# Batch 1's attention split into two groups inside tile 0, a later key-value product for batch 2, and q copies shared with ScalarE

## The chip, the cores and the metric

The kernel runs on one core of a Trainium2 chip. A core has five engines with a queue of instructions each: TensorE (PE, matmuls; PEld are its weight loads), VectorE (DVE), ScalarE (ACT), GpSimd (POOL) and SyncE (SP, which here only issues DMAs). The engines run side by side and wait for each other through semaphores. The metric is the device time of one execution in microseconds, the median of several runs.

## What is computed

Inputs are q, k, v of shape (8 batches, 8 heads, 576 rows, 64) and two weight matrices, 512 x 2048 and 2048 x 512. Cut to what matters:

```python
q_s = softmax(q, axis=-1)            # over the 64 entries of a row
k_s = softmax(k, axis=2)             # over the 576 rows
kv = einsum('bhsd,bhse->bhde', k_s, v)
x = einsum('bhsd,bhde->bhse', q_s, kv)          # "attention", linear in the rows
x = x.transpose(0, 2, 1, 3).reshape(4608, 512)
h = x @ w_in
out = maximum(0.01 * h, h) @ w_out              # 4608 x 512, float32
```

## The kernel before, in words

The 4608 rows are cut into nine tiles of 512 rows, and eight batches of 576 rows supply them. Tile 0 needs batch 0 alone: its layer 1 runs over all 576 rows of batch 0 (first rows 0 to 255, then the 320 others), and the 64 rows too many are carried over to tile 1. Tile 1 then needs the 448 rows behind those, which are the first of batch 1. For tile t >= 1 the body is a loop over 16 column blocks j of layer 1 (`layer1`, line 459, four matmuls each into one PSUM bank; then `leaky` on ScalarE, line 469), then four groups of 128 rows (`tsub`) with 16 layer-2 matmuls each (`layer2`, line 481), each group copied to SBUF and written out by `store` (line 474).

Attention for batch b goes through these steps: maximum of k over the rows (`k_tree`, `k_allmax`, VectorE), subtraction (`k_sub`), exponential (`k_exp`, ScalarE), cast of v (`v_cast`), and the same for q (`q_max`, `q_sub`, `q_exp`, `q_sum`, `q_norm`). `kv` (line 291) is the key-value product: 36 small matmuls into two PSUM banks, half of them for each half of v. `kd_make` (line 309) divides it by k's sums and leaves the matrix kd. q is needed transposed. For batch 0 TensorE does this (`q_transpose`, line 393, into a PSUM tile `psum_qt`) and `q_keep` (line 409) copies it to SBUF, into one tile for each pair of heads (`qT0`, `qT1`; argument `ggs`). From batch 1 on a DMA does it (`q_turn`, line 436). Then attention proper: `attend` (line 417, batch 0) or `attend_x` (line 444, other batches, eight matmuls: four pairs of heads g by two row ranges XR of 320 and 256 rows), each into a PSUM bank and from there, as bf16, into xT, which layer 1 reads. The engine of this copy is an argument.

PSUM has eight banks: two in the pool `psO` and six in `psB` (line 67). In tile 0 layer 2 runs with j outside and the four row groups inside, so that four output sums are open at once: two in `psO`, two in `psB`.

The order of the work is written out by hand. Each engine's queue gets its instructions in the order in which the program issues them. The main loops call `run(t, u)` after step u of tile t, and `at(t, u, ...)` (line 493) registers what is to be issued there. In tile 0 steps 0 to 15 are the column blocks for rows 0 to 255, 16 to 31 those for the other rows, 32 to 47 the j of layer 2. In later tiles 0 to 15 are the column blocks and 16 to 31 are layer 2, four j to a step, so that steps 20 to 23 are the second row group. Within one step the order of registration decides. Before the first loop, layer 1's first halves for blocks 0 to 7 are begun (`begin`, line 659); those for blocks 8 to 15 are begun at j = 8, between the two transposes of batch 0's late rows (lines 673 to 679).

The lines that the change touches: batch 0's late attention (584 to 586), batch 1's attention (597 to 599), batch 2's product and kd (635, 636), `g_carry` (656; eight GpSimd copies of the 64 carried rows), and the `q_keep` calls at j = 8 (677, 679).

Of the kernel before, what the change touches and what calls it, by code (L numbers as in the profile page):

```python
# [25 lines left out]
def kernel(  # L26
# [9 lines left out]
    nc = tc.nc  # L36
# [31 lines left out]
    psO_pool = ctx.enter_context(tc.tile_pool(name="psO", bufs=2, space=bass.MemoryType.PSUM))  # L68
# [75 lines left out]
    def k_begin(b):  # L144
        st[b]["ke"] = ke_pool.tile([P, R, HL, D], BF16, name="ke")
        st[b]["kmax"] = mx_pool.tile([P, HL, D], FP32, name="kmax")
        st[b]["kmaxT"] = mx_pool.tile([P, HL * D], FP32, name="kmaxT")
        st[b]["kall"] = mx_pool.tile([P, HL, D], FP32, name="kall")

    def k_tree(b, hs, steps=slice(0, 4)):  # L150
        n = hs.stop - hs.start
        ks = st[b]["k"][:, hs]
        if steps.start == 0:
            st[b]["t4"] = mx_pool.tile([P, HL, 4, D], FP32, name="t4")[:, 0:n]
        t4 = st[b]["t4"]
        t2, t1 = t4[:, :, 0:2], t4[:, :, 0]
        for o, i0, i1 in (
            (t4, ks[:, :, 0:4], ks[:, :, 4:8]),
            (t2, t2, t4[:, :, 2:4]),
            (t1, t1, t4[:, :, 1]),  # L160
            (st[b]["kmax"][:, hs], t1, ks[:, :, 8]),
        )[steps]:
            nc.vector.tensor_tensor(out=o, in0=i0, in1=i1, op=ALU.max)  # L163

    def k_allmax(b):


        nc.vector.transpose(
            out=st[b]["kmaxT"], in_=st[b]["kmax"].rearrange("p h d -> p (h d)")
        )  # L170
        m2 = small_pool.tile([P, CB, 2], FP32, name="m2")
        nc.vector.tensor_reduce(
            out=m2[:, :, 0],
            in_=st[b]["kmaxT"].rearrange("p (c j) -> p c j", j=32),
            axis=AX.X,
            op=ALU.max,
        )
        for a in range(4):
            o = a ^ 1
            nc.vector.tensor_reduce(  # L180
                out=m2[32 * o : 32 * o + 32, :, 1],
                in_=m2[32 * a : 32 * a + 32, :, 0:1],
                axis=AX.X,
                op=ALU.max,
            )
        m = small_pool.tile([P, CB], FP32, name="m")
        nc.vector.tensor_reduce(out=m, in_=m2, axis=AX.X, op=ALU.max)
        nc.vector.transpose(  # L188
            out=st[b]["kall"].rearrange("p h d -> p (h d)"),
            in_=m.unsqueeze(2).to_broadcast([P, CB, 32]),  # L190
        )
# [27 lines left out]
    def q_begin(b):  # L219
        st[b]["qe"] = qe_pool.tile([P, R, HL, D], BF16, name="qe")  # L220
        if b == 0:
            for gg in range(2):
                st[b]["qT", gg] = qT_pool.tile([P, 2, R, L], BF16, name=f"qT{gg}", tag="qT")
# [67 lines left out]
    def kv(b):  # L291

        pkv = [psB_pool.tile([P, 2, 130], FP32, name="pkv", tag=BANK_TAG) for _ in range(2)]
        for gg in range(2):
            for r in range(R):
                for hh in range(2):
                    rows = slice(hh * L, (hh + 1) * L)
                    nc.tensor.matmul(  # L298
                        pkv[hh][:, gg, 0:129],
                        lhsT=st[b]["ke"][rows, r, 2 * gg : 2 * gg + 2].rearrange(  # L300
                            "p h d -> p (h d)"
                        ),
                        rhs=vb2[b % 2][rows, r, gg, 0:129],
                        start=(r == 0),
                        stop=(r == R - 1),
                    )
        st[b]["pkv"] = pkv

    def kd_make(b):
        for hh in range(2):  # L310
            pkv = st[b]["pkv"][hh]
            krec = small_pool.tile([P, 2, 1], FP32, name="krec")
            nc.vector.reciprocal(out=krec, in_=pkv[:, :, 128:129])
            for hp in range(2):
                p0 = hp * D
                nc.vector.tensor_tensor(
                    out=kd2[b % 2][p0 : p0 + D, 2 * hh : 2 * hh + 2, p0 : p0 + D],
                    in0=pkv[p0 : p0 + D, :, p0 : p0 + D],
                    in1=krec[p0 : p0 + D].to_broadcast([D, 2, D]),
                    op=ALU.mult,  # L320
                )
# [87 lines left out]
    def q_keep(eng, b, r0, n, ggs=(0, 1)):  # L409
        for gg in ggs:  # L410
            o, i = st[b]["qT", gg][:, :, r0 : r0 + n], st[b]["ps", r0][:, gg::2]
            if eng is nc.scalar:
                eng.copy(out=o, in_=i)
            else:
                eng.tensor_copy(out=o, in_=i)

    def attend(b, gs, c0, n, eng, pool=psB_pool, tag=BANK_TAG):

        ps = pool.tile([P, len(gs), n], FP32, name="po", tag=tag)
        for i, g in enumerate(gs):  # L420
            nc.tensor.matmul(
                ps[:, i],
                lhsT=kd2[b % 2][:, g],
                rhs=st[b]["qT", g % 2][:, g // 2].rearrange("c r l -> c (r l)")[:, c0 : c0 + n],
                start=True,
                stop=True,
            )
        x0 = XB[gs[0]]
        o = xT[:, x0 : x0 + len(gs), b * S + c0 : b * S + c0 + n]
        if eng is nc.scalar:  # L430
            eng.copy(out=o, in_=ps)
        else:
            eng.tensor_copy(out=o, in_=ps)
# [10 lines left out]
    def attend_x(b, g, rs, eng):  # L444
        hh, gg = divmod(g, 2)
        n = (rs.stop - rs.start) * L
        ps = psB_pool.tile([P, n], FP32, name="po", tag=BANK_TAG)
        qX = st[b]["qX"].rearrange("c (r g) (h l) -> c g h r l", g=2, h=2)
        nc.tensor.matmul(  # L449
            ps.rearrange("p (r l) -> p r l", l=L), lhsT=kd2[b % 2][:, g], rhs=qX[:, gg, hh, rs]  # L450
        )
        c0 = b * S + rs.start * L
        o = xT[:, XB[g], c0 : c0 + n]
        if eng is nc.scalar:
            eng.copy(out=o, in_=ps)  # L455
        else:
            eng.tensor_copy(out=o, in_=ps)
# [35 lines left out]
    def at(t, u, *fns):  # L493
        while t > 0 and u >= 32:
            t, u = t + 1, u - 32
        hooks.setdefault((t, u), []).extend(fns)
# [14 lines left out]
    XR = (slice(0, 5), slice(5, R))  # L511
# [69 lines left out]
        load_w_out(slice(j0, j1))  # L581


    at(0, 11, lambda: attend(0, [0, 2], 256, 256, nc.scalar))
    at(0, 11, lambda: attend(0, [1, 3], 256, 256, nc.vector))
    at(0, 11, lambda: attend(0, [0, 2, 1, 3], 512, 64, nc.scalar, psO_pool, "pout"))
    at(0, 15, lambda: k_begin(1), lambda: q_begin(1), lambda: k_tree(1, H0), lambda: k_tree(1, H1))
    at(0, 15, lambda: q_max(1, XR[0]), lambda: q_sub(nc.gpsimd, 1, XR[0]), lambda: k_allmax(1))
    at(0, 15, lambda: k_sub(nc.vector, 1, H0), lambda: k_sub(nc.vector, 1, H1))
# [5 lines left out]
    at(0, 39, lambda: kv(1), lambda: q_sum(1, XR[1]), lambda: q_norm(1, XR[1]), lambda: kd_make(1))  # L595
    at(0, 43, lambda: q_turn(1, XR[1]), lambda: load_all(2))
    for i in range(8):
        eng = nc.vector if i in (5, 7) else nc.scalar
        at(0, 47, lambda i=i, eng=eng: attend_x(1, i % 4, XR[i // 4], eng))


    for b in range(3, B):
# [20 lines left out]
    def plan2():  # L623
        b = 2
        at(1, 0, lambda: k_begin(b), lambda: q_begin(b), lambda: k_tree(b, ALLH))
        at(1, 3, lambda: k_allmax(b))
        at(1, 6, lambda: k_sub(nc.vector, b, H0), lambda: k_sub(nc.vector, b, H1))
        at(1, 12, lambda: k_exp(b, ALLH))
        for rs in XR:
            at(1, 9, lambda rs=rs: q_max(b, rs), lambda rs=rs: q_sub(nc.gpsimd, b, rs))  # L630
        at(1, 13, lambda: v_cast(nc.gpsimd, b, 0), lambda: v_cast(nc.gpsimd, b, 1))
        for i, rs in enumerate(XR):
            at(1, (15, 16)[i], lambda rs=rs: q_exp(b, rs), lambda rs=rs: q_sum(b, rs), lambda rs=rs: q_norm(b, rs))
            at(1, (16, 17)[i], lambda rs=rs: q_turn(b, rs))
        at(1, 21, lambda: kv(b))
        at(1, 22, lambda: kd_make(b))
        for i in range(8):
            at(1, 28 + i // 2, lambda i=i: attend_x(b, i % 4, XR[i // 4], nc.scalar))

# [13 lines left out]
            g_next.append(g_tile())  # L653
            nc.gpsimd.tensor_copy(out=g_next[jj][:, :, 0:L], in_=g_sb[jj][:, :, TT : TT + L])

    at(0, 46, g_carry)
    begun = []

    def begin(j):
# [12 lines left out]
    for j in range(0, NF, 2):  # L672
        if j == 8:
            q_transpose(0, 4, 2)
            for jj in range(8, NF, 2):
                begin(jj)
            q_keep(nc.vector, 0, 4, 2)
            q_transpose(0, 6, 3)
            q_keep(nc.vector, 0, 6, 3)
        ph = begun.pop(0)  # L680
        for i in range(2):
            layer1(j + i, ph[:, i], 0, 256, slice(2, 4), i == 0, i == 1)
            if i == 1:
                leaky(g_sb[j // 2][:, :, 0:256], ph)
            run(0, j + i)
# [5 lines left out]
    pout = [psO_pool.tile([P, O], FP32, name="pout") for _ in range(2)]  # L691
# [66 lines left out]
```

## Time and profile before

| what | us |
|---|---|
| median of 3 runs (lowest, highest) | 291.18 (291.14, 291.42) |
| the profiled execution, its own time | 291.04 |
| its span, first to last instruction | 289.2 |
| TensorE busy | 279.7 |
| VectorE, ScalarE, GpSimd busy | 148.5, 148.2, 85.6 |

In the timeline's rows the columns are the start in us from the span's start, the time from the group's start to its end, engine, line, operation, what it writes and reads, the shapes, the number of instructions merged into the row, and in brackets the idle time of the engine just before with what ended it. Rows of the waits give the total in us, the number and the longest. Rows of the chain are the work that ended last, in order of time: start, duration, what. Matmuls overlap, so a group's duration contains the drain of its last matmul, and the next group can start before it ends.

### The profile page before, as it was taken

The numbers are of one execution on the slowest core, as the hardware profiler recorded it, in microseconds if no ns is written. First come the engines' busy times: TensorE is split into PE (matmuls) and PEld (weight loads), VectorE is DVE, ScalarE is ACT, GpSimd is POOL, SyncE is SP. The second block draws the span as 40 slices with busy tenths as digits, with TensorE's granted clock in tenths as the row PEclk, the third lists the DMA queues.
The fourth block names the chain that finished last, engine by engine and source line by source line (L and its number), as shares of the span: only waits on it lengthen the run. The fifth ranks groups of instructions, "written<-read, shape, count | busy, mean of one in ns | idle before, by whom it ended". The sixth has DMA issues, their size and how long they took to land.

```text
span 289.2 us, 4274 instructions
## 1 busy us (share of the span) xinstructions
PE 279.7 (97%) x1646; PEld 138.5 (48%) x1646; DVE 148.5 (51%) x246; ACT 148.2 (51%) x273; POOL 85.6 (30%) x70
## 2 busy tenths in 40 slices
PE   7689999999999999999999999999999999999995
PEld 2277654454444544454454544444454444444443
DVE  3997883896880994388175637554631200110011
ACT  4976870785269307922774358433953066016400
POOL 4735460017059009505900590039100000000000
PEclk9999999999999999999999999999999999999999
DMA  7999996987749174953397239913141310131033
GB/s 257 314 208 378 258 189 186 399 293 296 148 108 399 62 154 118 398 133 76 78 381 187 50 82 348 239 36 73 39 82 36 75 36 1 36 82 29 0 72 75
DMA packets 38932, 46.35 MB, mean 160 GB/s; under 512 B 18304, under 2 KB 21632, under 8 KB 38912
## 3 DMA queue, kind: packets, MB, share of 16 engines
q1 hardware_dynamic: 35456, 41.75, 48.5%
q0 software_dynamic: 3296, 4.20, 8.3%
q8 instruction: 13, 0.21, 0.3%
q10 hardware_dynamic: 160, 0.13, 0.1%
q14 instruction: 7, 0.06, 0.1%
HBM read 36.70 MB, written 9.44 MB: 160 GB/s over the span
## 4 chain that ended last, share of the span: by engine, by line
PE 74%; POOL 1%; ACT 0%; DVE 0%; issue 0%
PE pout L482 37%; PE ph L461 34%; PE pkv L298 2%; PE po L449 2%; POOL vb L216 1%; ACT xT L455 0%; DVE out_sb L476 0%
## 5 line engine op out<-in xcount | busy, mean ns | idle before, releaser
L482 PE MATMUL pout<-w_out_sb,gj 128*128 128x512 bf16 (+2 forms) x592 | 130.0, 373 | 0.0
L461 PE MATMUL ph<-xT,w_in_sb 128*128 128x512 bf16 (+3 forms) x640 | 127.5, 358 | 1.2 <-DMA w_in_sb<-in_moe_w_in_dram 0.7
L470 ACT ACTIVATE gj<-ph 128x512 bf16<-128x512 f32 (+2 forms) x152 | 83.6, 581 | 57.8 <-PE ph L461 55.8
L461 PEld LDWEIGHTS <-w_in_sb 128*128 128x128 bf16 x640 | 62.1, 98 | 63.5 <-issue 2.4
L482 PEld LDWEIGHTS <-gj 128*128 128x128 bf16 x592 | 57.0, 98 | 62.5
L476 DVE COPY out_sb<-pout 128x512 f32<-128x512 f32 (+1 forms) x34 | 22.7, 675 | 85.4 <-PE pout L482 82.5
L196 POOL TENSOR_TENSOR k_raw<-k_raw,kall 128x2304 f32<-128x2304 f32 x5 | 25.3, 5066 | 76.8 <-DVE kall L188 50.4
L455 ACT CAST xT<-po 128x320 bf16<-128x320 f32 (+1 forms) x54 | 18.8, 405 | 48.4 <-PE po L449 48.4
L259 POOL TENSOR_TENSOR q_raw<-q_raw,qmax 128x2304 f32<-128x2304 f32 (+3 forms) x10 | 29.7, 2974 | 22.4 <-DVE qmax L228 22.4
L276 DVE TENSOR_REDUCE qsum<-qe 128x36 f32<-128x2304 bf16 (+4 forms) x11 | 19.8, 1798 | 32.2 <-ACT qe L267 32.2
L283 DVE TENSOR_TENSOR qe<-qe,qrec 128x2304 bf16<-128x2304 bf16 (+4 forms) x12 | 21.9, 1826 | 0.4
L204 ACT ACTIVATE ke<-k_raw 128x2304 bf16<-128x2304 f32 (+2 forms) x11 | 17.5, 1595 | 8.7 <-POOL k_raw L196 8.5
L228 DVE TENSOR_REDUCE qmax<-q_raw 128x36 f32<-128x2304 f32 (+4 forms) x11 | 19.6, 1788 | 0.0
L267 ACT ACTIVATE qe<-q_raw 128x2304 bf16<-128x2304 f32 (+4 forms) x11 | 16.8, 1526 | 1.5 <-POOL q_raw L259 1.3
L216 POOL CAST vb<-v_raw 128x1152 bf16<-128x1152 f32 x13 | 14.6, 1147 | 0.0
L449 PE MATMUL po<-qX,kd 128*128 128x320 bf16 (+1 forms) x56 | 11.6, 286 | 0.3
L163 DVE TENSOR_TENSOR t<-k_raw 128x1024 f32<-128x1024 f32 (+1 forms) x10 | 10.1, 1011 | 0.5 <-DMA k_raw<-in_k_dram 0.2
L327 PE MATMUL pout<-zero 128*128 128x512 bf16 x28 | 8.9, 443 | 1.3 <-POOL zero L101 1.3
L163 DVE TENSOR_TENSOR t<-t 128x256 f32<-128x256 f32 (+2 forms) x20 | 9.6, 478 | 0.7
L476 ACT COPY out_sb<-pout 128x512 f32<-128x512 f32 (+1 forms) x3 | 1.6, 543 | 15.6 <-PE pout L482 15.6
L298 PE MATMUL pkv<-vb,ke 64*128 64x129 bf16 x252 | 8.5, 216 | 0.4 <-POOL vb L216 0.4
L298 PEld LDWEIGHTS <-ke 64*128 64x128 bf16 x252 | 7.2, 93 | 3.5 <-ACT gj L470 1.7
(61 smaller groups left out, 100.3 us busy)
## 6 DMA issues: line engine op xcount, KB each, us to landing
out_dram<-out_sb SPq DMA_DIRECT2D x70, 128.0 KB, 2.4
q_raw<-in_q_dram SPq DMA_DIRECT2D x7, 1152.0 KB, 8.2
v_raw<-in_v_dram SPq DMA_DIRECT2D x7, 1152.0 KB, 11.5
k_raw<-in_k_dram SPq DMA_DIRECT2D x6, 1152.0 KB, 5.8
k_raw<-in_k_dram SPq DMA_DIRECT2D x4, 576.0 KB, 5.6
w_in_sb<-in_moe_w_in_dram POOLq DMA_DIRECT2D x8, 256.0 KB, 7.1
v_raw<-in_v_dram SPq DMA_DIRECT2D x2, 576.0 KB, 7.4
w_out_sb<-in_moe_w_out_dram POOLq DMA_DIRECT2D x4, 256.0 KB, 9.4
```

The source lines that it names most:

```text
L163: nc.vector.tensor_tensor(out=o, in0=i0, in1=i1, op=ALU.max)
L196: eng.tensor_tensor(out=ks, in0=ks, in1=st[b]["kall"][:, hs].unsqueeze(2).to_broadcast([P, n, R, D]), op=ALU.subtract,)
L228: nc.vector.tensor_reduce(out=m, in_=st[b]["q"][:, :, rs], axis=AX.X, op=ALU.max)
L259: eng.tensor_tensor(out=qs, in0=qs, in1=st[b]["qmax", rs.start].unsqueeze(3).to_broadcast([P, HL, n, D]), op=ALU.subtract,)
L276: nc.vector.reduce_sum(out=qsum, in_=st[b]["qe"][:, rs], axis=AX.X)
L283: nc.vector.tensor_tensor(out=qes, in0=qes, in1=st[b]["qrec", rs.start].unsqueeze(3).to_broadcast([P, n, HL, D]), op=ALU.mult,)
L298: nc.tensor.matmul(pkv[hh][:, gg, 0:129], lhsT=st[b]["ke"][rows, r, 2 * gg : 2 * gg + 2].rearrange("p h d -> p (h d)"), rhs=vb2[b % 2][row ...
L455: eng.copy(out=o, in_=ps)
L461: nc.tensor.matmul(ph, lhsT=w_in_sb[:, cb, j * P : (j + 1) * P], rhs=xT[:, XB[cb], c0 : c0 + n], start=(i == 0 and first), stop=(i == NB - ...
L470: nc.scalar.activation(out=o, in_=ph, func=AF.Prelu, alpha=LEAKY_SLOPE)
L476: copy(out=out_sb, in_=pout)
L482: nc.tensor.matmul(pout, lhsT=g_sb[j // 2][:, j % 2, tsub * P : (tsub + 1) * P], rhs=w_out_sb[:, j, os], start=(j == 0), stop=(j == NF - 1),)
```

## The change

Batch 0's late attention is issued two steps earlier, after block 9. Batch 1's eight attention matmuls are no longer issued together after the last step of tile 0's layer 2, but four after j = 13 and four after j = 14; their copies alternate between ScalarE and VectorE, in the order of head pairs 0, 2, 1, 3. Batch 2's key-value product and kd are issued two steps later in tile 1. `g_carry` is issued one step later. Of the two copies out of each transposed block of batch 0's late rows, ScalarE takes the one for the first pair of heads; VectorE keeps the second.

```diff
-    at(0, 11, lambda: attend(0, [0, 2], 256, 256, nc.scalar))
-    at(0, 11, lambda: attend(0, [1, 3], 256, 256, nc.vector))
-    at(0, 11, lambda: attend(0, [0, 2, 1, 3], 512, 64, nc.scalar, psO_pool, "pout"))
+    at(0, 9, lambda: attend(0, [0, 2], 256, 256, nc.scalar))
+    at(0, 9, lambda: attend(0, [1, 3], 256, 256, nc.vector))
+    at(0, 9, lambda: attend(0, [0, 2, 1, 3], 512, 64, nc.scalar, psO_pool, "pout"))
...
     for i in range(8):
-        eng = nc.vector if i in (5, 7) else nc.scalar
-        at(0, 47, lambda i=i, eng=eng: attend_x(1, i % 4, XR[i // 4], eng))
+        eng = (nc.scalar, nc.vector)[i % 2]
+        at(0, (45, 46)[i // 4], lambda i=i, eng=eng: attend_x(1, (0, 2, 1, 3)[i % 4], XR[i // 4], eng))
...
-        at(1, 21, lambda: kv(b))
-        at(1, 22, lambda: kd_make(b))
+        at(1, 23, lambda: kv(b))
+        at(1, 24, lambda: kd_make(b))
...
-    at(0, 46, g_carry)
+    at(0, 47, g_carry)
...
-            q_keep(nc.vector, 0, 4, 2)
+            q_keep(nc.scalar, 0, 4, 2, (0,))
+            q_keep(nc.vector, 0, 4, 2, (1,))
             q_transpose(0, 6, 3)
-            q_keep(nc.vector, 0, 6, 3)
+            q_keep(nc.scalar, 0, 6, 3, (0,))
+            q_keep(nc.vector, 0, 6, 3, (1,))
```

## The prediction

> **What bounds the kernel now.** First the page: shares of busy time, the slices of TensorE (PE) and the clock, the shares of the chain that ended last.
>
> ```profile
> span 289.2 us, 4274 instructions
> PE 279.7 (97%) x1646; PEld 138.5 (48%) x1646; DVE 148.5 (51%) x246; ACT 148.2 (51%) x273; POOL 85.6 (30%) x70
> ...
> PEclk9999999999999999999999999999999999999999
> ...
> PE 74%; POOL 1%; ACT 0%; DVE 0%; issue 0%
> ```
>
> TensorE is busy for 97% of the span at full clock, and the chain is TensorE from 70.6 us to the end. A microsecond of TensorE idleness that goes is a microsecond of the kernel, as long as its next operand is there. So I look for holes in TensorE's row. A busy share hides them, because matmuls are pipelined and their modelled ends overlap the next start; I take the times at which groups start. The waits of TensorE and the chain come next, then the timeline at the places that the diff touches.
>
> ```profile
> PE pkv L298 <- POOL vb L216: 0.4, 1, 0.4
> PE ph L461 <- ACT xT L431: 0.2, 1, 0.2
> ```
>
> ```profile
> 68.41 2.19 POOL vb L216 x2
> 70.60 0.04 issue
> 70.64 0.69 PE pkv L298 x18
> ...
> 77.48 0.27 PE po L449 x2
> 77.75 0.86 PE pout L482 x4
> ...
> 79.75 0.22 PE po L449 x2
> ```
>
> The first wait is batch 2's key-value product, which stands still until GpSimd (POOL) has cast the second half of v at 70.60; there the chain leaves TensorE. The second is tile 0's layer 1 waiting for batch 0's late attention. The chain also gives two prices: four layer-2 matmuls take 0.86 us, and a pair of attention matmuls 0.27 (320 wide) or 0.22 (256 wide).
>
> **Part one: batch 1's attention.** The end of tile 0 in the timeline:
>
> ```profile
> 46.82 0.29 POOL L654 COPY gj<-gj 128x128 bf16<-128x128 bf16 x1 [1.44 <-PE pout L482]
> ...
> 49.95 2.07 PE L449 MATMUL po<-qX,kd 128*128 128x320 bf16 x8
> 50.29 1.97 ACT L455 CAST xT<-po 128x320 bf16<-128x320 f32 x6 [8.44 <-PE po L449]
> ...
> 51.40 0.42 DVE L457 CAST xT<-po 128x256 bf16<-128x256 f32 x1 [5.21 <-PE po L449]
> ...
> 52.03 8.19 PE L461 MATMUL ph<-xT,w_in_sb 128*128 128x448 bf16 x42
> ...
> 52.40 2.47 DVE L476 COPY out_sb<-pout 128x512 f32<-128x512 f32 x4
> ...
> 54.91 1.23 DVE L163 TENSOR_TENSOR t<-k_raw 128x1024 f32<-128x1024 f32 x1
> ```
>
> The eight matmuls start at 49.95 and layer 1 of tile 1 at 52.03: 2.08 us. By the chain's pairs they need 2 x 0.27 + 2 x 0.22 = 0.98. The other 1.10 is a wait for PSUM: two of the six general banks hold output sums, four are left, and the fifth matmul waits until ScalarE (ACT), at 0.33 us a copy (1.97 / 6), has emptied the first.
>
> After the change four of them stand behind layer 2's j = 13 and four behind j = 14. Without a shift from earlier parts, j = 14 begins at 49.95 - 2 x 0.86 = 48.23. The first four run 48.23 to 48.77, j = 14 to 49.63, the second four to 50.07, j = 15 to 50.93, and layer 1 can follow there. First copies begin 0.34 after their matmul (50.29 against 49.95): ScalarE 48.57 to 49.00 and 48.90 to 49.33. VectorE (DVE) copies 320 wide are not in this trace. They lie between 0.42 (256 wide, above) and 0.69 (512 wide, below); I take 0.49, by width, nearest to 0.42: done at about 49.2 and 49.65. The second four want their banks at 49.63, 49.74, 49.85 and 49.96, all free. Their copies end by about 50.9, and layer 1 reads the last of them only after several matmuls. So I cost the attention at its 0.98 and the wait at nothing: **-1.10**. The cover is layer 2. With 0.69 a copy the fourth bank is free at 50.0, and up to 0.1 to 0.2 comes back; in the other direction there may be 0.1 more, as layer 1's second matmul also waited.
>
> The operands: batch 1's kd is made long before, and the second half of the transposed q lands in time (the transpose and the load behind it on SyncE's queue, then the landings of batch 1's two transposes):
>
> ```profile
> 44.72 1.23 SPq L439 DMA_TRANSPOSE qX<-qe  x1
> 46.06 0.52 SPq L79 DMA_DIRECT2D k_raw<-in_k_dram  x1
> ```
>
> ```profile
> DMA to landing us min/median/max: 3.1/3.4/3.6
> ```
>
> 44.72 + 3.6 = 48.3, wanted at 49.63. SyncE's and GpSimd's queues keep their order in the built program. The carry of g moved from step 46 to 47 passes nothing on GpSimd; its copies still wait for layer 2's readers alone (the last at 46.82), and tile 1's activations start after 51.
>
> VectorE is also free sooner: its last attention copy ends near 50.9, so the four output copies run about 50.9 to 53.4 and batch 2's max tree begins near 53.4, not 54.91. This **1.5 us** matters next. Its k has landed (46.06 + 5.7 = 51.8):
>
> ```profile
> k_raw<-in_k_dram SPq DMA_DIRECT2D x2, 1152.0 KB, 5.7
> ```
>
> **Part two: batch 2's key-value product.** The timeline there, and the same product for batch 3:
>
> ```profile
> 64.22 5.34 PE L482 MATMUL pout<-w_out_sb,gj 128*128 128x512 bf16 x24
> ...
> 69.55 0.69 PE L298 MATMUL pkv<-vb,ke 64*128 64x129 bf16 x18
> ...
> 70.64 0.69 PE L298 MATMUL pkv<-vb,ke 64*128 64x129 bf16 x18 [0.41 <-POOL vb L216]
> ...
> 71.26 6.22 PE L482 MATMUL pout<-w_out_sb,gj 128*128 128x512 bf16 x28
> ...
> 75.55 0.59 DVE L316 TENSOR_TENSOR kd<-pkv,krec 64x128 bf16<-64x128 f32 x2
> ...
> 77.32 0.44 PE L449 MATMUL po<-qX,kd 128*128 128x320 bf16 x2
> ```
>
> ```profile
> 99.41 1.20 PE L298 MATMUL pkv<-vb,ke 64*128 64x129 bf16 x36
> ...
> 100.54 7.08 PE L482 MATMUL pout<-w_out_sb,gj 128*128 128x512 bf16 x32
> ```
>
> From first product matmul to the next layer-2 matmul it takes 71.26 - 69.55 = 1.71 for batch 2, 100.54 - 99.41 = 1.13 for batch 3: 0.58 of standing. Two steps later are eight layer-2 matmuls, 1.72. The 24 matmuls from 64.22 would end at 69.4, so the product starts at 71.1 on the old clock, about 70.0 after part one. The second half of v is wanted 0.56 later, at 70.6. It is cast at 70.60 even if GpSimd gains nothing, and at about 69.1 if batch 2's chain moves by 1.5. **-0.58**, with some 0.05 more at its front. The price would be kd: it ended at 76.14 because VectorE was busy with q, not because of the product, and attention wants it at 77.32 - 1.68 = 75.64. Moved by 1.5 it is there at 74.6.
>
> **Part three: batch 0's late attention and q's copies.**
>
> ```profile
> 14.88 0.58 ACT L413 COPY qT<-psum_qt 128x512 bf16<-128x512 bf16 x1 [0.60 <-PE psum_qt L397]
> ...
> 15.60 0.42 DVE L415 COPY qT<-psum_qt 128x512 bf16<-128x512 bf16 x1
> ```
>
> ```profile
> 23.60 0.62 DVE L415 COPY qT<-psum_qt 128x384 bf16<-128x384 bf16 x2 [0.94 <-PE psum_qt L397]
> ...
> 23.69 1.03 PE L461 MATMUL ph<-xT,w_in_sb 128*128 128x256 bf16 x8
> 24.32 1.08 ACT L470 ACTIVATE gj<-ph 128x512 bf16<-128x512 f32 x2 [2.91 <-PE ph L461]
> ...
> 24.56 0.72 PE L421 MATMUL po<-qT,kd 128*128 128x256 bf16 x8
> ...
> 25.20 0.69 DVE L433 CAST xT<-po 128x512 bf16<-128x512 f32 x1 [0.97 <-PE po L421]
> 25.29 0.87 ACT L431 CAST xT<-po 128x512 bf16<-128x512 f32 x2
> ```
>
> Now VectorE has both copies of the last rows done at 24.22, and attention starts at 24.56 without a wait. Afterwards four layer-1 matmuls fewer stand ahead: at 0.11 each ((24.56 - 23.69) / 8) attention could start at 24.12. ScalarE copies one pair of heads, VectorE the other, but not side by side: in the built program VectorE's copy waits for ScalarE's. ScalarE's 384-wide copy is not in the trace. Above it stands 0.58 (512 wide, 14.88), below it VectorE's 0.31 for the same width (0.62 / 2); I take 0.50, nearer to the same engine's row. So ScalarE copies from 23.60 to 24.10, and VectorE, at 0.31 and a little for the hand-over, until about 24.5. The first two matmuls go at 24.15, the next two wait from 24.37 to about 24.55: some 0.2 of new standing. What goes is the 0.2 for which layer 1 waited for ScalarE's xT copies, since twelve layer-1 matmuls and not eight now cover them. **0.0**, between +0.1 (0.58) and -0.2 (no new wait). Behind ScalarE's copy is queued the activation that could not start before 24.32 anyway, with 2.91 us idle before it; behind VectorE's is its xT copy, then batch 1's max tree, neither later than now.
>
> The Trainium skill, page "PSUM — Partial Sum Buffer", section "PSUM bank collisions raise a hardware error", says that ScalarE and VectorE may not read one bank's partitions at once, and that software must order them. The rows at 14.88 and 15.60, the same split for the first rows, agree: 14.88 + 0.58 ends before 15.60. By this rule the term stays at 0.0; with the two copies side by side it would be about -0.2.
>
> **The sum.** -1.10 - 0.58 + 0.0 = -1.68. The profiled execution took 291.04 (span 289.2 and 1.8 around it), so 289.36; the runs' median, 291.18, is 0.14 higher, so about 289.5. The small terms left out (0.1 and 0.05) point down: I say **289.4**. Behind the product the chain hardly leaves TensorE (its 74% are nearly all that the span has after 70.64), so nothing later takes the gain back unless a new wait opens.
>
> **Rivals.**
> *Batch 2 does not follow (8%).* If its chain of VectorE, GpSimd and ScalarE stays where it is, kd comes at 76.14 and TensorE, due at 75.64, stands 0.5 us: 289.4 + 0.5 = 289.9 to 290.0. For it: kd comes at the end of a long chain over three engines, and any link bound by something else stays. Against it: it begins behind VectorE's output copies, which move by 1.5.
> *The attention is only half hidden (10%).* If the second four wait for VectorE's copies and layer 1 for the last of them, 0.3 to 0.7 of the 1.10 stays: 289.7 to 290.1. For it: VectorE takes twice the copies, two in width never seen. Against it: 0.86 us of layer 2 between the groups, against 0.33 to 0.5 per copy on two engines.
> *The transpose is late (4%): slower.* Group two puts a DMA ahead of layer 2's last four matmuls. The landings over the whole trace:
>
> ```profile
> DMA to landing us min/median/max: 3.0/4.5/6.8
> ```
>
> At 6.8, q lands at 51.5 and TensorE stands 1.9 from 49.63: 291.18 - 1.68 + 1.9 = 291.4. It decides from a landing of 6.6 us on. Against it: 6.8 is from whole transposes; this half took 3.1 to 3.6.
> *The change does little (6%).* TensorE's holes close there and open elsewhere, in layer 1 behind banks held by output sums, say: 290.7 to 291.3.
>
> **Chances.** The forecast has 72%, with 289.1 to 289.7 as its own range. 0.2%, about 0.6 us, is what a measurement of this kernel can tell from no change. Forecast and the first two rivals are faster by more: 0.90. The small change is the 0.06 within, the late transpose the 0.04 beyond (most of it only just). The range runs from 288.9 (the sum with 0.2 of part three, the small terms and a little scatter) to 290.2 (the first two rivals' upper ends).
>
> **What would show it.** The eight batch-1 matmuls as two groups of 0.54 and 0.44 with 0.86 between, and 448-wide layer 1 within 0.1 of layer 2's end; no wait of the product for GpSimd, and 1.13 from its start to the next layer-2 matmul; batch 2's max tree on VectorE about 1.5 earlier; TensorE's wait for ScalarE's xT gone and a wait of some 0.2 for q's copies in its place, with 320-wide layer 1 still starting near 26.2. It is wrong if TensorE stands at step 46 or before batch 2's attention, or if layer 1 of tile 1 is no earlier than 51.2.

## The result, and the profile after

The changed kernel takes 289.64 us (median of 6 runs, 288.84 to 289.88), the kernel before in the same comparison 291.10 (290.98 to 291.42). The ratio is 0.9941 with a 95% interval of 0.9931 to 0.9951: faster by 1.4 to 2.0 us, where 289.4 was forecast. The profiled execution took 289.65.

The same lines of the page after as were shown of before:

```profile
span 287.8 us, 4248 instructions
PE 277.4 (96%) x1620; PEld 138.6 (48%) x1646; DVE 148.9 (52%) x246; ACT 148.1 (51%) x273; POOL 85.6 (30%) x70
...
PEclk9999999999999999999999999999999999999999
...
PE 90%; DMA 3%; issue 1%; DVE 1%; POOL 1%; ACT 0%; ACTq 0%; POOLq 0%
```

Only 1620 of TensorE's 1646 matmuls are recorded here, but all 1646 weight loads. A lost record of a 512-wide matmul looks like a hole of about 0.22 us in its row; a real hole has a late weight load beside it. TensorE's waits after:

```profile
PE ph L461 <- DMA w_in_sb<-in_moe_w_in_dram: 1.2, 2, 0.8
...
PE ph L461 <- ACT xT L431: 0.2, 1, 0.2
```

The wait of the product for GpSimd is gone. The wait for w_in (the first weight matrix; blocks 8 to 15 use the half that is loaded second), 0.7 before, is now 1.2. The wait for xT is the same one in both kernels, 0.24 in tile 0's first blocks, at 16.57 before and 16.80 after; it was never that for batch 0's late attention. The latter has no row among the waits. It shows as a hole of 0.24 in TensorE's weight loads, where the 320-wide layer 1 begins. Before:

```profile
16.57 0.60 PE L461 MATMUL ph<-xT,w_in_sb 128*128 128x256 bf16 x4 [0.24 <-ACT xT L431]
```

```profile
26.22 1.86 PEld L461 LDWEIGHTS <-w_in_sb 128*128 128x128 bf16 x14 [0.24 <-issue]
```

The second hole ends 0.06 behind ScalarE's late copies to xT (25.29 + 0.87 = 26.16). After, the loads run through:

```profile
25.31 2.66 PEld L461 LDWEIGHTS <-w_in_sb 128*128 128x128 bf16 x23
```

The timeline of TensorE and VectorE at the end of tile 0:

```profile
48.66 0.71 PE L449 MATMUL po<-qX,kd 128*128 128x320 bf16 x4
...
49.14 0.89 DVE L457 CAST xT<-po 128x320 bf16<-128x320 f32 x2 [2.51 <-PE po L449]
49.21 1.03 PE L482 MATMUL pout<-w_out_sb,gj 128*128 128x512 bf16 x4
...
50.07 0.60 PE L449 MATMUL po<-qX,kd 128*128 128x256 bf16 x4
...
50.51 1.03 PE L482 MATMUL pout<-w_out_sb,gj 128*128 128x512 bf16 x4
...
51.16 2.47 DVE L476 COPY out_sb<-pout 128x512 f32<-128x512 f32 x4
51.37 3.95 PE L461 MATMUL ph<-xT,w_in_sb 128*128 128x448 bf16 x20
```

The groups take 0.55 and 0.44 with 0.86 between, and layer 1 of tile 1 starts 0.86 after layer 2's last four begin: nothing stands, that is, TensorE waits nowhere here. Further on, TensorE's row alone from layer 2 of tile 0 to tile 2:

```profile
35.34 7.07 PE L482 MATMUL pout<-w_out_sb,gj 128*128 128x512 bf16 x31
...
51.37 12.27 PE L461 MATMUL ph<-xT,w_in_sb 128*128 128x448 bf16 x64
...
70.48 1.20 PE L298 MATMUL pkv<-vb,ke 64*128 64x129 bf16 x36
71.61 4.49 PE L482 MATMUL pout<-w_out_sb,gj 128*128 128x512 bf16 x19
...
79.51 3.69 PE L461 MATMUL ph<-xT,w_in_sb 128*128 128x512 bf16 x14
```

The same stations before:

```profile
34.91 7.07 PE L482 MATMUL pout<-w_out_sb,gj 128*128 128x512 bf16 x32
...
52.03 12.35 PE L461 MATMUL ph<-xT,w_in_sb 128*128 128x448 bf16 x64
...
80.89 2.40 PE L461 MATMUL ph<-xT,w_in_sb 128*128 128x512 bf16 x9
```

From layer 2's start to tile 1: 17.12 before, 16.03 after, -1.09. From tile 1 to tile 2: 28.86 and 28.14, -0.72. From tile 2 to the end: 289.2 - 80.89 and 287.8 - 79.51, both 208.3. That is -1.81 from layer 2 on. Ahead of it the profiled execution after is 0.43 later, so the two spans differ by only 1.4.

These 0.43 are not the change's. Kernels with the same code up to there start layer 2 at different times, as the second half of w_in comes: among the profiles below, attention alone at 34.73 and the late chain at 35.84, which do not differ before 53 us. So each kernel below is also read from layer 2's start, where this scatter is out.

### The profile page after: what moved, and what is told of

The parts are those of the page before. It is cut to its first block, busy times and chain, and to the rows that moved or that the text cites. A ratio compares the mean times of both kernels' runs of the same rounds, so it can differ in the third digit from the quotient of the medians.

```text
span 287.8 us, 4248 instructions
## 1 busy us (share of the span) xinstructions
PE 277.4 (96%) x1620; PEld 138.6 (48%) x1646; DVE 148.9 (52%) x246; ACT 148.1 (51%) x273; POOL 85.6 (30%) x70
## 4 chain that ended last, share of the span: by engine, by line
PE 90%; DMA 3%; issue 1%; DVE 1%; POOL 1%; ACT 0%; ACTq 0%; POOLq 0%
PE pout L482 43%; PE ph L461 41%; DMA w_in_sb<-in_moe_w_in_dram 3%; PE pkv L298 3%; PE po L449 2%; DVE k_raw L364 1%; POOL w_in_sb L134 0%; ACT gj L470 0%; PE po L421 0%; ACT xT L455 0%; DVE out_sb L476 0%; POOL gate L546 0%; ACTq L470 0%; POOLq L546 0%
## 5 line engine op out<-in xcount | busy, mean ns | idle before, releaser
L455 ACT CAST xT<-po 128x320 bf16<-128x320 f32 (+1 forms) x52 | 18.2, 402 | 48.6 <-PE po L449 48.6
L449 PEld LDWEIGHTS <-kd 128*128 128x128 bf16 x56 | 5.5, 98 | 6.2
```

What stands on the lines that cost most here:

```text
L449: nc.tensor.matmul(ps.rearrange("p (r l) -> p r l", l=L), lhsT=kd2[b % 2][:, g], rhs=qX[:, gg, hh, rs])
```

## The experiments

All times are against the kernel before on the same chip in the same comparison. Its medians are 291.10 for the changed kernel, 291.16 for the first set (attention, product and late rows alone, and the change without late rows), 291.24 for one group, ScalarE's copies and the two late chains, 290.96 for the last three. Across sets the ratios are to be compared, not the medians. "From layer 2" is the time from layer 2's start to that of tile 1 and from there to that of tile 2, in each kernel's profile, and their sum against before.

| kernel | median | ratio, 95% interval | layer 2 starts | from layer 2 | against before |
|---|---|---|---|---|---|
| before | | | 34.91 | 17.12 + 28.86 | |
| changed | 289.64 | 0.9941 [0.9931, 0.9951] | 35.34 | 16.03 + 28.14 | -1.81 |
| attention alone | 289.44 | 0.9934 [0.9921, 0.9948] | 34.73 | 16.03 + 28.28 | -1.67 |
| product alone | 290.34 | 0.9968 [0.9955, 0.998] | 34.92 | 17.12 + 28.22 | -0.64 |
| late rows alone | 291.09 | 0.9998 [0.9988, 1.0007] | 34.90 | 17.12 + 28.87 | 0.0 |
| changed without late rows | 289.38 | 0.9929 [0.9914, 0.9944] | 35.57 | 16.03 + 28.13 | -1.82 |
| one group | 289.78 | 0.9949 [0.9936, 0.9963] | 34.80 | 16.70 + 28.13 | -1.15 |
| copies on ScalarE | 289.52 | 0.9949 [0.9936, 0.9962] | 35.12 | 16.10 + 28.13 | -1.75 |
| attention alone, chain late | 290.72 | 0.9985 [0.9974, 0.9995] | 35.84 | 16.03 + 29.53 | -0.42 |
| attention, product, chain late | 289.38 | 0.994 [0.9928, 0.9953] | 35.23 | 16.02 + 28.14 | -1.82 |
| changed, q copies on VectorE | 289.13 | 0.993 [0.9917, 0.9944] | 35.11 | 16.02 + 28.14 | -1.82 |
| changed, batch 2's attention | 288.92 | 0.993 [0.9917, 0.9943] | 34.75 | 16.03 + 28.14 | -1.81 |
| the same, w_in sooner | 288.93 | 0.9922 [0.9908, 0.9935] | 34.88 | 16.03 + 28.13 | -1.82 |

**Attention alone.** The kernel before with this:

```diff
-        eng = nc.vector if i in (5, 7) else nc.scalar
-        at(0, 47, lambda i=i, eng=eng: attend_x(1, i % 4, XR[i // 4], eng))
+        eng = (nc.scalar, nc.vector)[i % 2]
+        at(0, (45, 46)[i // 4], lambda i=i, eng=eng: attend_x(1, (0, 2, 1, 3)[i % 4], XR[i // 4], eng))
...
-    at(0, 46, g_carry)
+    at(0, 47, g_carry)
```

> The kernel before with batch 1's attention in its two groups (steps 45 and 46, g_carry at 47) and nothing else. Theory A, the prediction's sum, in which each part pays for itself: -1.1 us, and TensorE's wait of the product for GpSimd's cast (0.4 in the waits of before) is still there, since the product is where it was. Rival B: the output copies on VectorE, and with them batch 2's whole chain up to the cast of v, move by more than TensorE does (in the profile of the changed kernel the cast starts at 67.12, not 68.41, although the profile's first 25 us are 0.4 later: about 1.7, against 1.1 for TensorE). Then 0.6 of 0.64 of the product's standing goes with the attention alone: -1.6 to -1.7, and no wait for the cast above 0.1 in TensorE's waits.

Its timeline at batch 2's product, GpSimd and TensorE:

```profile
66.51 2.24 POOL L216 CAST vb<-v_raw 128x1152 bf16<-128x1152 f32 x2
...
68.14 1.34 PE L298 MATMUL pkv<-vb,ke 64*128 64x129 bf16 x36
...
69.64 4.70 PE L482 MATMUL pout<-w_out_sb,gj 128*128 128x512 bf16 x21 [0.16 <-issue]
```

The product stands at its old step 21, but the 36 matmuls now run in one piece of 1.34, against 1.20 without any wait: 0.14 is left of the standing. (The 0.16 behind them is a lost record: the first layer-2 matmul's weight load is there.) The median is 1.7 below before, and 1.67 shows from layer 2 on. Rival B is right.

**Product alone.** The kernel before with this:

```diff
-        at(1, 21, lambda: kv(b))
-        at(1, 22, lambda: kd_make(b))
+        at(1, 23, lambda: kv(b))
+        at(1, 24, lambda: kd_make(b))
```

> The kernel before with batch 2's product and kd two steps later and nothing else. Both theories: the cast's end does not move (70.6) and the product wants its second half at about 71.7, so -0.58 to -0.64, and 1.13 from its first matmul to the next of layer 2. If kd came late by it, part of this would be seen as a gap of TensorE before 77.3.

TensorE's row there:

```profile
71.23 1.20 PE L298 MATMUL pkv<-vb,ke 64*128 64x129 bf16 x36
72.36 4.49 PE L482 MATMUL pout<-w_out_sb,gj 128*128 128x512 bf16 x19
```

1.13 from start to layer 2, and -0.64: as both expected, 0.58 of standing and 0.06 at the product's front. The price of the wait was right; alone, the move takes it.

**Late rows alone, and the change without them.** The first is the kernel before with attention for batch 0 at step 9 and ScalarE's share of the copies; the second is the changed kernel with these lines as before:

```diff
-    at(0, 11, lambda: attend(0, [0, 2], 256, 256, nc.scalar))
+    at(0, 9, lambda: attend(0, [0, 2], 256, 256, nc.scalar))
...
-            q_keep(nc.vector, 0, 6, 3)
+            q_keep(nc.scalar, 0, 6, 3, (0,))
+            q_keep(nc.vector, 0, 6, 3, (1,))
```

> The kernel before with batch 0's late attention at step 9 and ScalarE's share of q's copies, and nothing else. Theory A, the prediction's: 0.0, TensorE's 0.2 of waiting for xT replaced by 0.2 of waiting for q's copies. Rival C: layer 1's blocks 8 and 9 wait for the second half of w_in for so long that q's copies are done under it (in the profile of the changed kernel TensorE starts them at 24.35, 0.4 after the copies' data were there, and attention follows without a wait); then only the 0.2 goes: -0.2. Layer 2 starts 0.0 (A) or 0.2 (C) earlier, counted from the end of the wait for w_in.

> The changed kernel without the third part (batch 0's late attention at step 11 and all of q's late copies on VectorE, as before). Theory A: -1.1 - 0.58 = -1.7, and 0.6 faster than attention alone. Rival B: the same as attention alone within 0.1. Under rival C for part three this kernel is 0.2 slower than the changed one; under the prediction's, equal to it.

The second kernel equals attention alone in time (289.38 and 289.44) and is 0.15 better from layer 2 on: B again. In the first, the median moves by -0.07, within its interval; the profile tells more. Its timeline:

```profile
23.23 0.48 ACT L413 COPY qT<-psum_qt 128x384 bf16<-128x384 bf16 x1 [1.19 <-PE psum_qt L397]
23.74 0.36 DVE L415 COPY qT<-psum_qt 128x384 bf16<-128x384 bf16 x1 [0.91 <-ACT qT L413]
```

```profile
23.91 0.60 PE L461 MATMUL ph<-xT,w_in_sb 128*128 128x256 bf16 x4 [0.71 <-DMA w_in_sb<-in_moe_w_in_dram]
24.34 0.72 PE L421 MATMUL po<-qT,kd 128*128 128x256 bf16 x8
...
34.90 1.46 PE L482 MATMUL pout<-w_out_sb,gj 128*128 128x512 bf16 x5
```

VectorE's copy starts when ScalarE's has ended, as the prediction had it. But TensorE came back from its wait for w_in only at 23.91, and both copies were done (24.10) before the second pair of attention matmuls wanted them. From there to layer 2: 34.90 - 23.91 = 10.99, against 34.91 - 23.69 = 11.22 before (11.21 or 11.22 in every kernel here without part three). So in this profile it is C, -0.23; layer 2 starts no earlier because TensorE came to blocks 8 and 9 later by 0.22. The times do not decide: the ratio's interval, 0.9988 to 1.0007, holds 0.0 and -0.23, and the change without late rows is no slower than the change (0.9929 and 0.9941).

**Copies on ScalarE, and part three without a late wait for w_in.** The changed kernel with `eng = nc.scalar` for all eight copies of batch 1's attention:

> The changed kernel with all eight copies of batch 1's attention on ScalarE. The prediction's theory (layer 2 between the groups covers four copies at 0.33): the same time as the changed kernel within 0.1. Rival, half-hidden attention: one engine is too slow for it, the second group or layer 1 of tile 1 waits 0.3 or more.

From layer 2 on it is 0.06 slower than the changed kernel, within the 0.1 expected, and its copies are one row of eight in 2.58. So VectorE's share of the copies buys almost nothing. In this execution TensorE waits for w_in only ahead of the transposes, not behind them, and the timeline shows the other face of part three:

```profile
21.59 1.91 PE L461 MATMUL ph<-xT,w_in_sb 128*128 128x256 bf16 x16 [0.69 <-DMA w_in_sb<-in_moe_w_in_dram]
23.33 0.50 PE L397 MATMUL psum_qt<-ident,qe 128*128 128x128 bf16 x6
23.96 0.60 PE L461 MATMUL ph<-xT,w_in_sb 128*128 128x256 bf16 x4
24.40 0.89 PE L421 MATMUL po<-qT,kd 128*128 128x256 bf16 x8
...
35.12 1.24 PE L482 MATMUL pout<-w_out_sb,gj 128*128 128x512 bf16 x4
```

No wait is noted at 23.96, and the eight attention matmuls take 0.89 in place of 0.72: 0.17 of waiting for the second copy. 35.12 - 23.96 = 11.16: against 11.22, part three gains 0.06. Counted from the transposes it is 35.12 - 23.33 = 11.79, against 34.91 - 23.07 = 11.84 in the kernel before, which does not wait for w_in behind them either: 0.05.

**The changed kernel with q's late copies on VectorE alone:**

```diff
-            q_keep(nc.scalar, 0, 6, 3, (0,))
-            q_keep(nc.vector, 0, 6, 3, (1,))
+            q_keep(nc.vector, 0, 6, 3)
```

(and the same for the rows before).

> The changed kernel with q's late copies back on VectorE alone; batch 0's attention stays at step 9. Rival C (the wait for w_in covers q's copies): the same as the changed kernel within 0.1, so ScalarE's share buys nothing and the 0.2 comes from the earlier attention. Its rival: the split shortens q's way, and without it attention waits 0.1 to 0.2 for the second copy. Counted from the end of the wait for w_in to layer 2's start: 10.99 us in the changed kernel, 11.22 in the one before.

```profile
24.12 0.60 PE L461 MATMUL ph<-xT,w_in_sb 128*128 128x256 bf16 x4 [0.35 <-DMA w_in_sb<-in_moe_w_in_dram]
24.55 0.72 PE L421 MATMUL po<-qT,kd 128*128 128x256 bf16 x8
25.10 10.17 PE L461 MATMUL ph<-xT,w_in_sb 128*128 128x256 bf16 x76
35.11 1.24 PE L482 MATMUL pout<-w_out_sb,gj 128*128 128x512 bf16 x5
```

10.99 again, so the 0.23 comes from the earlier attention and not from ScalarE's share. The two copies on VectorE take 0.62 together here as before; ScalarE's 0.48 and VectorE's 0.36 in turn took 0.87 (23.23 to 24.10). TensorE waited for w_in behind the transposes in this execution, so what VectorE alone does without that wait was not seen. From the two durations the second copy would end 0.25 sooner (0.87 - 0.62), and the 0.17 above would go: an estimate.

**One group.** The changed kernel with all eight at step 46:

```diff
-        at(0, (45, 46)[i // 4], lambda i=i, eng=eng: attend_x(...))
+        at(0, 46, lambda i=i, eng=eng: attend_x(...))
```

> The changed kernel with all eight of batch 1's attention matmuls at step 46 (one group ahead of j = 15), the copies still alternating. The prediction's theory, four free PSUM banks: the fifth to eighth matmul each wait for a copy, about 0.6 in all (first copy done 0.8 after the group's start, the fourth 1.45, against 0.54 and 0.87 without waiting), so 0.5 to 0.6 slower than the changed kernel. Rival: the alternating copies and the place ahead of layer 2 suffice, and the split into groups buys nothing: 0.0 to 0.1.

```profile
48.98 1.81 PE L449 MATMUL po<-qX,kd 128*128 128x320 bf16 x8
50.64 1.02 PE L482 MATMUL pout<-w_out_sb,gj 128*128 128x512 bf16 x4
51.50 12.27 PE L461 MATMUL ph<-xT,w_in_sb 128*128 128x448 bf16 x64
```

```profile
49.80 0.42 PEld L449 LDWEIGHTS <-kd 128*128 128x128 bf16 x3 [0.31 <-issue]
```

1.66 for the eight, against 0.98: from layer 2's start it is 0.67 slower than two groups, though the copies alternate. (The ratios, 0.9949 and 0.9941, do not show it; their intervals overlap.) Five weight loads run through; the sixth comes only at 49.80, when the fifth matmul starts. By then ScalarE's first copy is done (it begins at 49.32 and takes 0.43). That is the wait for the four banks, and layer 2 between the groups is the cover. A kernel with more free banks was not made.

**The chain held back.** Attention alone, and attention with the later product (no late rows), each with the first step of batch 2's max tree done twice on VectorE:

```diff
-        at(1, 0, lambda: k_begin(b), lambda: q_begin(b), lambda: k_tree(b, ALLH))
+        at(1, 0, lambda: k_begin(b), lambda: q_begin(b), lambda: k_tree(b, ALLH, slice(0, 1)), lambda: k_tree(b, ALLH))
```

> Attention alone (the kernel before with batch 1's attention in two groups), with the first step of batch 2's max tree done twice: 1.23 us more on VectorE at the start of batch 2's chain, output unchanged. Rival B, by which the product's wait went because that chain moved further than TensorE: the cast of v ends 1.2 later and the product stands for it again, 1.2 to 1.4: 1.2 slower than attention alone. Theory A, by which the chain's start does not matter for the product: no change against attention alone.

> Attention and the later product, without part three, with the same 1.23 us more on VectorE, output unchanged. Rival B: the two later steps (1.72) cover the cast's 1.2, so no wait of the product; kd comes close to batch 2's attention, 0.0 to 0.2 slower than the same kernel without the addition, and about 1.1 faster than attention alone with the addition. Theory A: the two differ by 0.58.

TensorE's row of the first:

```profile
70.06 0.69 PE L298 MATMUL pkv<-vb,ke 64*128 64x129 bf16 x18 [0.74 <-POOL vb L216]
71.15 0.69 PE L298 MATMUL pkv<-vb,ke 64*128 64x129 bf16 x18 [0.40 <-POOL vb L216]
72.00 5.99 PE L482 MATMUL pout<-w_out_sb,gj 128*128 128x512 bf16 x27 [0.16 <-issue]
```

And of the second:

```profile
70.36 1.20 PE L298 MATMUL pkv<-vb,ke 64*128 64x129 bf16 x36
71.49 4.49 PE L482 MATMUL pout<-w_out_sb,gj 128*128 128x512 bf16 x19
75.82 0.43 PE L449 MATMUL po<-qX,kd 128*128 128x320 bf16 x2
```

With 1.23 more on VectorE the product stands again, 0.74 and 0.40 in its waits, and attention alone loses 1.25 between tile 1 and tile 2. With the later product the same delay costs nothing, at the product or at batch 2's attention. So the product's time is tied to VectorE's start, and the later product is a margin of at least 1.2 us, of which this kernel needs 0.14.

**Batch 2's attention, and w_in sooner.** The changed kernel with batch 2's last pair a step earlier, then the same with one GpSimd copy removed that holds back the second half of w_in:

```diff
-            at(1, 28 + i // 2, lambda i=i: attend_x(b, i % 4, XR[i // 4], nc.scalar))
+            at(1, (28, 29, 30, 30)[i // 2], lambda i=i: attend_x(b, i % 4, XR[i // 4], nc.scalar))
...
-    nc.gpsimd.tensor_copy(out=gate[:, 0:1], in_=st[0]["k"][:, HL - 1, R - 1, D - 1 : D])
     load_w_in(8, 16)
```

> The changed kernel with batch 2's last pair of attention matmuls one step earlier (both pairs of the short rows at step 30 of tile 1, so that layer 2's last four matmuls cover the copies). In the changed kernel layer 1 of tile 2 stands 0.3 after its first matmul for the last pair's copies. If this hole is treated like the one at the end of tile 0: -0.3 against the changed kernel. If a new wait takes its place (four banks, the transpose's landing): 0.0 or slower.

> The kernel before this one in the list (changed, batch 2's attention earlier), with the second half of w_in no longer held back on GpSimd until VectorE has subtracted k's maximum; the issue moves 0.9 earlier. If that load alone sets the start of blocks 8 and 9: 0.3 to 0.9 faster, and q's copies are then no longer covered, so a wait for them of 0.1 to 0.3 appears. If the load only shares its bandwidth with the loads before it: 0.0 or slower.

TensorE's weight loads at the start of tile 2, in the changed kernel:

```profile
79.40 0.21 PEld L461 LDWEIGHTS <-w_in_sb 128*128 128x128 bf16 x2
80.02 2.90 PEld L461 LDWEIGHTS <-w_in_sb 128*128 128x128 bf16 x14 [0.42 <-issue]
```

And with batch 2's attention earlier:

```profile
78.70 4.20 PEld L461 LDWEIGHTS <-w_in_sb 128*128 128x128 bf16 x20
```

The hole is gone. It lies behind tile 2's start: from there to batch 3's product it is 97.14 - 78.92 = 18.22, and 98.03 - 79.51 = 18.52 in the changed kernel, so -0.30 as expected. The median is 288.92, against 290.96 for the kernel before in this comparison. The changed kernel's ratio, 0.9941, lies within this one's interval, so the times alone do not show the 0.30.

With w_in sooner as well the median is 288.93: nothing that the times can tell. Its row from the transposes on:

```profile
23.09 0.50 PE L397 MATMUL psum_qt<-ident,qe 128*128 128x128 bf16 x6
23.56 0.60 PE L461 MATMUL ph<-xT,w_in_sb 128*128 128x256 bf16 x4
24.15 0.89 PE L421 MATMUL po<-qT,kd 128*128 128x256 bf16 x8
...
34.88 1.46 PE L482 MATMUL pout<-w_out_sb,gj 128*128 128x512 bf16 x6
```

The kernel without this edit has the transposes at 22.96, blocks 8 and 9 at 23.55, attention at 24.02 (0.89 too) and layer 2 at 34.75. So blocks 8 and 9 come 0.47 behind the transposes' start in place of 0.59, but attention then waits for the first of q's copies as well, 0.59 behind blocks 8 and 9 in place of 0.47. From the transposes to layer 2 both take 11.79: what w_in gave, q took.

## Why the prediction was right, and which step of it was not

- **Attention at the end of tile 0, -1.10.** Measured -1.09, with the groups and the starts as worked out. VectorE's 320-wide copy, taken at 0.49, shows as two in 0.89. The cause was tested: without the two groups 0.67 comes back, without VectorE's share 0.06. The order of the head pairs and the later carry of g are in every kernel with the new attention; no run tests them apart. Layer 1 of tile 1 runs through as well, 12.27 against 12.35: the 0.1 that the prediction named and left out is 0.08, so TensorE gains 1.17.
- **VectorE 1.5 sooner.** It was 1.67 (52.40 - 34.91 against 51.16 - 35.34, from layer 2's start to the output copies). The output copies began close to 50.7 on the old clock, not 50.9.
- **The product, -0.58: the step that failed.** The size of the wait was right (0.64 when the product alone is moved). To price the move at it on top of part one was not. Part one moves TensorE by 1.17, but the chain that ends in the cast of v by 1.67; the wait of 0.64 for that cast shrinks by the difference, 0.50, to 0.14 by itself. The prediction had both numbers, 1.5 and 1.10, in its hand and used the 1.5 only to show that the later product was safe. So attention is worth 1.67, and the product's move 0.14 on top (1.81 - 1.67), not 1.10 and 0.58. In the other order the price holds: the product's move alone is worth 0.64, and attention on top of it 1.18 (1.82 - 0.64). The sum does not notice, since both orders end at the same point where nothing stands.
- **Part three, 0.0.** Right as the likely value when TensorE does not wait for w_in behind the transposes: the new wait for q's copies is 0.17 (0.2 forecast), the gain 0.05 in all three such profiles. When it does, as in the changed kernel's own profile, the copies lie under that wait and the gain is 0.23, near the prediction's lower bound of -0.2; so the wait for q's copies that the prediction named as a sign does not appear there. That w_in decides it was not seen. The 0.2 that goes was read from the wrong row, the wait at 16.57, which stays; that the right hole, at 26.22, has the same size is luck. ScalarE's 384-wide copy, taken at 0.50, took 0.48. The rule of the Trainium skill cited there (page "PSUM — Partial Sum Buffer", section "PSUM bank collisions raise a hardware error"), that the two engines may not read a bank's partitions at once, agrees with these profiles: VectorE's copy out of the split bank starts behind ScalarE's end in each of them, and the split makes the pair 0.25 longer (0.87 against 0.62). No run let the two overlap.
- **The sum.** -1.68 was forecast; -1.81 is measured from layer 2 on in the profile. The median moved by 1.46, and the ratio's interval, 1.4 to 2.0, holds 1.68 and 1.81. The start-up, whose scatter is larger than the smaller terms, accounts for 0.43 in the profiled execution; for the medians it can only be supposed, as one execution of each kernel is profiled.
- **The rivals.** Batch 2 followed, and had slack: 1.2 more on its chain did no harm once the product was late. The half-hidden attention and the late transpose did not occur, and no other hole took the gain back. A kernel with a late transpose was not made.

## What to carry to other kernels

When two waits of the busiest engine hang on one chain, price the second again after the first is gone: if the chain behind the second starts at the place that the first sets free, the second wait may go with it, and two gains become one. A wait for PSUM banks is removed by other work of TensorE between groups of as many outputs as there are free banks, and a second engine for the copies matters less (0.67 and 0.06 here). A split of one bank's copy over two engines was a queue of two (0.87 against 0.62).

## What had not been expected

Layer 2 of tile 0 starts anywhere from 34.73 to 35.84 us in profiles of kernels whose code is the same up to the DMA of w_in and the late rows. It follows the time at which TensorE gets the second half of w_in (0.6 of waiting in one profile, 1.3 in another): from the end of the wait behind the transposes to layer 2 it is 11.21 or 11.22 without part three and 10.99 with it, in every profile that has that wait. The range is over 1 us, more than the third part of the change can bring, so such terms are read in the profile between two stations and not in the median.
